# First stage of the spectral branch: kernel half rounded before signal half from row 4 on, last two rows convolved one by one

## The chip, the cores and the metric

One core of a Trainium2 chip runs the whole program. The metric is the device time in microseconds of one execution; the number given is the median of several runs.

## What is computed

The input `x` has 2048 rows (sequence) of 576 channels. Four layers follow each other, each added to its input after a layer norm: a Fourier mix (A), a gated state-space branch (B), A again, B again. B does not look at its input's layers at all beyond the gate: its expensive part depends on `k`, `v` and the weights only.

```python
def _A_ref(x, dft_seq_re, dft_seq_im, dft_hid_re, dft_hid_im):
    a = jnp.einsum("bsd,ed->bse", x, dft_hid_re)
    b = jnp.einsum("bsd,ed->bse", x, dft_hid_im)
    return jnp.einsum("ts,bse->bte", dft_seq_re, a) - jnp.einsum("ts,bse->bte", dft_seq_im, b)

def _B_ref(q, k, v, shift_k, ssm_k, ssm_D):
    k_pad = jnp.pad(k, ((0, 0), (ks - 1, 0), (0, 0)))
    k_shift = sum(k_pad[:, t:t + S, :] * shift_k[:, ks - 1 - t] for t in range(ks))   # ks = 4
    kv = k_shift * v
    y = irfft(rfft(kv, 2 * S) * rfft(ssm_k, 2 * S))[:S] + kv * ssm_D
    return q * y

x = x + _A_ref(_layernorm(x), ...)
x = x + _B_ref(_layernorm(x), ...)
x = x + _A_ref(_layernorm(x), ...)
x = x + _B_ref(_layernorm(x), ...)
```

## The kernel before

**The main line.** Each A layer is two rounds of matrix products on TensorE. In the first layer (`layer`) the sequence product runs over 128 steps: for each of 4 blocks of output rows and 2 matrices (cosine, sine), 16 steps over the contraction. One step multiplies the normalised rows by one 128x512 tile of the DFT matrix. Every fp32 number is carried as a rounded part and a remainder, so a step is 12 products into four accumulators `s` and 2 into `rm`. The tile of the DFT matrix arrives by a DMA from SyncE's queue (L171), ScalarE rounds it (`mats<-flts`, L101) and VectorE subtracts to get the remainder (`mats<-flts,mats`, L102). This last one is called a C split below. Two steps are prepared ahead.

**The branch.** The B layers share one inverse and forward transform of `k_shift * v` and `ssm_k`. It runs between the steps of the first layer, as a generator (`branch`) that the main loop advances by a few pieces per step. The positions are 16 rows `j` of 128x576 numbers each. The first stage, which the change touches, does for each row:

- the signal half: convolve `k` with the four taps of `shift_k` (`convolve`, L397 multiplies and L402 adds, two rows at a time on a 128x1152 view, 7 operations for a pair), multiply by the row of `v` (L430), round on ScalarE (`f1r<-f1f`, L101), subtract on VectorE (`f1r<-f1f,f1r`, L102);
- the kernel half: the row of `ssm_k` is loaded (L422), rounded (`f1r<-flts`, L101) and subtracted (`f1r<-flts,f1r`, L102);
- from row 4 on, one set of products for both halves: three visits (`f1_products`), each 6 matmuls of 128x384 into two of three PSUM banks `bf`, then two ScalarE copies out of the banks (L455, called evacuations below) and a store to DRAM from ScalarE's queue (L456).

**What sets the order.** `todo` lists (row, half) in the order in which the halves are rounded; 1 is the kernel half, 0 the signal half. Rows 0 to 3 do all kernel halves, then all signal halves. From row 4 on it goes signal, kernel, signal, kernel. Each entry gives two slots in the main loop. The convolution's operations are spread over these slots: `left` is the number of operations that must be done before the next signal half, divided by the slots until then. `f1_loads` asks for the rows of `v` and `ssm_k` three entries ahead, into a ring of three buffers (`land`): a load waits until the entry three places before it has been read for the last time. The three visits of a row follow the rounding of its second half. On top of this a scheduler places the instructions of each engine; every engine, and SyncE's queue of loads too, then works strictly in that order.

The rest of the program (hidden product, middle stage of the branch, the third layer with Strassen's scheme, the gates) is not touched.

Of the kernel before, what the change touches and what calls it, by code (L numbers as in the profile page):

```python
# [13 lines left out]
OP = mybir.AluOpType  # L14
# [4 lines left out]
D = 576  # L19
J = S // P  # L20
# [11 lines left out]
K_FIRST = 4  # L32
# [22 lines left out]
KR = 4  # L55
# [13 lines left out]
def fnet_h3_kernel(ctx: ExitStack, tc: tile.TileContext, x, c_mat, w_re, w_im, k_pad, v, shift_k,  # L69
                   ssm_k, ssm_d, f1c, i2c, midc, out):  # L70
    nc = tc.nc
# [28 lines left out]
    def split(h, l, src):  # L100
        a = nc.scalar.activation(h, src, AF.Copy).ins  # L101
        return a, nc.vector.tensor_tensor(l, src, h.bitcast(F32), OP.subtract).ins  # L102
# [31 lines left out]
    def lay(t, at, *sizes):  # L134

        for name, words, n in sizes:
            ring.setdefault(name, Ring()).tiles.extend(t[:, at + i * words:at + (i + 1) * words] for i in range(n))
            at += n * words
        assert at <= t.shape[1], (at, t.shape, sizes)
        return at  # L140
# [5 lines left out]
    def two(v):  # L146
        return v.rearrange("p (a n) -> p a n", a=2)
# [198 lines left out]
    def parts(i):  # L346
        v = ring[i]()
        return v[:, :D], v[:, D:]
# [4 lines left out]
    def branch():  # L353
# [3 lines left out]
        at = lay(flts, SC_AT + CRAW * NT, ("so", D, 4), ("land", D, 3))  # L357
# [3 lines left out]
        ks = f1f[:, :KR * 2 * D]  # L361
        lay(f1f, KR * 2 * D, ("wt", 2 * D, 2), ("rp", 2 * D, 2))
        tmp = f1f[:, 8 * 2 * D:]
        wt, rows, landed, fcs, paired = [], {}, {}, {}, []
        k_loaded = [0]

        def load_w4():
            for i in range(2):
                t = two(ring["wt"]())
                nc.sync.dma_start(t, bass.AP(tensor=shift_k.tensor, offset=shift_k.offset + 2 * i * D,  # L370
                                             ap=[[0, P], [D, 2], [1, D]]))
                wt.extend(t[:, i, :].unsqueeze(1).broadcast_to([P, 2, D]) for i in range(2))

        def load_k(upto):
            while k_loaded[0] < min(upto, (J + 4) // 2):
                i = k_loaded[0]
                at = i % KR * 2 * D
                nc.sync.dma_start(ks[:, at:at + 2 * D], k_pad[:, 2 * i * D:2 * (i + 1) * D])
                k_loaded[0] += 1

        def k_rows(row):

            at = row % (2 * KR) * D
            if at + 2 * D <= KR * 2 * D:
                return [(slice(0, 2), two(ks[:, at:at + 2 * D]))]
            return [(slice(n, n + 1), ks[:, o:o + D].unsqueeze(1)) for n, o in ((0, at), (1, 0))]

        def convolve():
            for i in range(J // 2):
                if not wt:  # L390
                    load_w4()
                load_k(i + KR - 1)
                rp = rows[i] = two(ring["rp"]())
                for t in range(4):
                    out_t = two(tmp) if t else rp
                    for n, k in k_rows(2 * i + t):
                        nc.vector.tensor_tensor(out_t[:, n], k, wt[3 - t][:, n], OP.mult)  # L397
                    yield
                    if t == 1:
                        load_k(i + KR)  # L400
                    if t:
                        nc.vector.tensor_tensor(rp, rp, out_t, OP.add)  # L402
                        yield

        todo = [(1, 1), (0, 1)] + [(j, 1) for j in range(2, K_FIRST)] + [(j, 0) for j in range(K_FIRST)]
        todo += [(j, src) for j in range(K_FIRST, J) for src in range(2)]
        loads = [0]

        def f1_loads(upto):
            while loads[0] < min(upto, len(todo)):  # L410
                j, src = todo[loads[0]]
                loads[0] += 1
                if j not in fcs:
                    fcs[j] = two(ring["fc"]())
                    if pows:
                        load_fr(fcs[j], f1c[j])
                    else:
                        raw = two(tmp[:, :2 * P])
                        nc.sync.dma_start(raw, f1c[j])
                        nc.scalar.activation(fcs[j], raw, AF.Copy)  # L420
                landed[j, src] = ring["land"]()
                nc.sync.dma_start(landed[j, src], (ssm_k if src else v)[:, j, :])  # L422
                if src and j == 0:
                    nc.sync.dma_start(tmp[:1, D:], ssm_d[None, :])

        def f1_split(j, src):
            r = landed.pop((j, src))
            if not src:
                row = rows[j // 2][:, j % 2, :]
                nc.vector.tensor_tensor(row, row, r, OP.mult)  # L430
                r = row
            elif j == 0:
                nc.vector.tensor_tensor(r[:1], r[:1], tmp[:1, D:], OP.add)
            if j < K_FIRST:
                xf = parts("xf")
                parted[:] = split(xf[0], xf[1], r)
                return xf
            if not src:
                t = ring["xp"]()
                paired[:] = t[:, :2 * D], t[:, 2 * D:]  # L440
            h, l = (t.rearrange("p (a s d) -> p a s d", a=2, s=2)[:, :, src, :] for t in paired)
            parted[:] = split(h, l, two(r))
            return tuple(paired)

        def f1_products(j, fc, xf, at, n, so, to):
# [10 lines left out]
            nc.scalar.dma_start(t_d[:, j::J, to:to + n], so)  # L456

        conv, made_ops, visits = convolve(), 0, []
        def visit(half):
            if visits and visits[0][0] <= half:  # L460
                f1_products(*visits.pop(0)[1:])

        for n, (j, src) in enumerate(todo):
            f1_loads(n + 1)
            if n < 2:
                yield
            xf = f1_split(j, src)
            if j < K_FIRST:
                visits += [(2 * n + 2, j, fcs[j], xf, hf * HD, HD, "so", hf * D + src * HD) for hf in range(2)]
            elif src:  # L470
                visits += [(2 * n + 3, j, fcs[j], xf, at, VW, "sp", at) for at in range(0, 2 * D, VW)]
            if n:
                f1_loads(n + 3)
            later = [m for m in range(n + 1, len(todo)) if todo[m][1] == 0 and 7 * (todo[m][0] // 2 + 1) > made_ops]
            for half in range(2):
                visit(2 * n + half)
                if later and n > 2:
                    left = 7 * (todo[later[0]][0] // 2 + 1) - made_ops
                    for _ in range(-(-left // (2 * (later[0] - n) - half)) if left > 0 else 0):
                        next(conv)  # L480
                        made_ops += 1
                yield
# [6 lines left out]
        at = lay(m1, 0, ("df", 2 * D, 3), ("mc", 4 * P, 1))  # L489
# [6 lines left out]
        at = lay(m1, at, ("yf", D, 2))  # L496
        fc_at = at
        at = lay(flts, SC_AT + CRAW * NT, ("res", D, 2))
# [267 lines left out]
    pending = []  # L766
    lay(flts, SC_AT, ("craw", NT, CRAW))
    br = branch()
    wl = load_w()
    load_x(0)  # L770
# [29 lines left out]
    for n, whole in layer(get_x0, lambda j: x[:, j, :], done0, pending):  # L800
        part = whole == "part"
        if part:
            whole = False
        if (whole or whole is not None and n % J < J - 1) and n <= F1_END and not part:
            at = n if whole else n - 0.5
# [27 lines left out]
        m = n - PREP  # L833
# [207 lines left out]
    for n, whole in layer(get_x1, lambda j: xb_d[j], done1, pending, 1):  # L1041
# [12 lines left out]
        if n == STATIC:  # L1054
            t7.append(region_a(FR, "t7"))
            at = lay(flts, SC_AT + CRAW * NT, ("csum", WIDE, 3), ("rems", 2 * REM, 2))
# [128 lines left out]
```

## Time and profile before

| | |
|---|---|
| median of 3 runs | 1179.39 us (1178.54 to 1179.56) |
| the profiled execution | 1178.94 us, of which 1177.0 us are the span from its first to its last instruction |
| TensorE matmul busy | 1165.9 us |
| VectorE busy | 867.8 us |
| ScalarE busy | 647.8 us |
| granted TensorE clock | 0.999 |

The first stage of the branch runs from the first microseconds to about 197 us; the rows with 384 columns, from row 4 on, take from about 92 us to 196 us. `PE` is the matmul part of TensorE, `PEld` its weight loads, `DVE` VectorE, `ACT` ScalarE, `SP` SyncE; `SPq` and `ACTq` are instructions of their queues, mostly DMA issues. A line of a timeline gives the start, the duration from the first start to the last end of a run of equal instructions, and in brackets the engine's idle time before it with what ended it.

### The profile page before, as it was taken

The numbers are of one execution on the slowest core, as the hardware profiler recorded it, in microseconds if no ns is written. First come the engines' busy times: TensorE is split into PE (matmuls) and PEld (weight loads), VectorE is DVE, ScalarE is ACT, GpSimd is POOL, SyncE is SP. The second block draws the span as 40 slices with busy tenths as digits, with TensorE's granted clock in tenths as the row PEclk, the third lists the DMA queues.
The fourth block names the chain that finished last, engine by engine and source line by source line (L and its number), as shares of the span: only waits on it lengthen the run. The fifth ranks groups of instructions, "written<-read, shape, count | busy, mean of one in ns | idle before, by whom it ended". The sixth has DMA issues, their size and how long they took to land.

```text
span 1177.0 us, 18134 instructions
## 1 busy us (share of the span) xinstructions
PE 1165.9 (99%) x6198; PEld 989.8 (84%) x6198; DVE 867.8 (74%) x1564; ACT 647.8 (55%) x1280; POOL 75.7 (6%) x115
## 2 busy tenths in 40 slices
PE   9999999999999999999999999999999999999997
PEld 6776667988899988898888898888888888889997
DVE  7899984688787788877757666866685777774674
ACT  8865655567766667766645667434434445450210
POOL 2310000000000000001101111000000000001111
PEclk9999999999999999999999999999999999999999
DMA  9879898546766766749966777772762877894531
GB/s 326 298 232 306 270 300 284 164 139 178 214 206 192 210 181 191 193 135 258 272 197 216 249 245 239 239 238 89 251 240 73 251 262 257 265 332 149 194 111 41
DMA packets 147453, 255.64 MB, mean 217 GB/s; under 512 B 16161, under 2 KB 56353, under 8 KB 147362
## 3 DMA queue, kind: packets, MB, share of 16 engines
q1 hardware_dynamic: 111890, 210.17, 56.6%
q10 hardware_dynamic: 28560, 37.91, 9.1%
q0 software_dynamic: 6912, 6.43, 2.4%
q8 instruction: 48, 0.79, 0.3%
q14 instruction: 43, 0.35, 0.1%
HBM read 187.80 MB, written 66.65 MB: 216 GB/s over the span
## 4 chain that ended last, share of the span: by engine, by line
PE 93%; DVE 2%; DMA 2%; ACT 1%; issue 1%; SPq 0%; POOL 0%; DVEq 0%; ACTq 0%
PE s L78 54%; PE bk L78 31%; PE rm L78 6%; PE bf L78 2%; DMA t<-ud 1%; DVE f1f L397 1%; DMA vd<-flts 0%; DVE f1f L402 0%; DVE mats L102 0%; DMA early<-in_x 0%; ACT flts L516 0%; DMA flts<-vd 0%; DMA td<-flts 0%; DVE f1r L102 0%; ACT mid L516 0%
## 5 line engine op out<-in xcount | busy, mean ns | idle before, releaser
L78 PE MATMUL s<-mats 128*128 128x512 f32 x2102 | 548.0, 396 | 2.7 <-DVE mats L762 1.5
L78 PEld LDWEIGHTS s<-mats 128*128 128x128 f32 x2102 | 382.7, 189 | 83.8 <-issue 10.9
L102 DVE TENSOR_TENSOR mats<-flts,mats 128x512 fp32r<-128x512 f32 x206 | 140.9, 688 | 55.8 <-ACT mats L101 53.4
L101 ACT ACTIVATE mats<-flts 128x512 fp32r<-128x512 f32 x206 | 128.2, 628 | 79.9 <-PE bk L78 29.6
L516 ACT ACTIVATE flts<-bk 128x288 f32<-128x288 f32 (+1 forms) x192 | 78.4, 409 | 97.7 <-PE bk L78 85.2
L78 PE MATMUL bk<-mid 128*128 128x288 f32 x704 | 127.9, 298 | 0.7 <-DVE mid L522 0.4
L78 PEld LDWEIGHTS bk<-mid 128*128 128x128 f32 x704 | 111.2, 188 | 19.7 <-ACT flts L516 4.5
L78 PE MATMUL bk<-w,u 128*128 128x288 f32 x864 | 120.5, 295 | 0.2
L78 PEld LDWEIGHTS bk<-w,u 128*128 128x128 f32 x864 | 116.8, 188 | 2.4 <-ACT flts L516 1.4
L522 DVE TENSOR_TENSOR mid<-flts,mid 128x576 fp32r<-128x576 f32 (+1 forms) x149 | 92.5, 625 | 7.4 <-ACT mid L516 5.3
L78 PE MATMUL rm<-mats 128*128 128x512 f32 x304 | 94.7, 391 | 0.0
L516 ACT ACTIVATE mid<-flts 128x576 fp32r<-128x576 f32 (+1 forms) x148 | 79.5, 574 | 1.9 <-DMA flts<-vd 0.9
L78 PE MATMUL bk<-mats 128*128 128x288 f32 (+1 forms) x376 | 67.8, 317 | 0.0
L78 PEld LDWEIGHTS rm<-mats 128*128 128x128 f32 x304 | 56.9, 188 | 12.5 <-issue 0.3
L455 ACT ACTIVATE flts<-bf 128x384 f32<-128x384 f32 (+1 forms) x104 | 43.2, 462 | 42.9 <-PE bf L78 40.5
L291 DVE TENSOR_TENSOR flts<-flts,bk 128x288 f32<-128x288 f32 x48 | 21.8, 454 | 60.6 <-PE bk L78 58.3
L78 PE MATMUL s<-t,mats 128*128 128x512 f32 x264 | 65.3, 390 | 0.3 <-DVE t L102 0.3
L188 POOL TENSOR_TENSOR flts<-flts 128x1 f32<-128x1 f32 x34 | 28.0, 824 | 517.0 <-DVE flts L187 517.0
L78 PE MATMUL bk<-mats,t 128*128 128x288 f32 (+1 forms) x368 | 59.3, 303 | 0.0
L78 PEld LDWEIGHTS s<-t,mats 128*128 128x128 f32 x264 | 49.4, 188 | 11.2 <-DVE t L102 0.8
L516 ACT ACTIVATE flts<-flts 64x288 f32<-64x288 f32 x128 | 56.7, 443 | 3.9
L78 PEld LDWEIGHTS bk<-mats 128*128 128x128 f32 x376 | 55.6, 188 | 3.4
(152 smaller groups left out, 1496.6 us busy)
## 6 DMA issues: line engine op xcount, KB each, us to landing
flts<-in_c_mat SPq DMA_DIRECT2D x148, 256.0 KB, 3.5
ph<-in_c_mat SPq DMA_DIRECT2D x54, 512.0 KB, 4.4
flts<-in_c_mat SPq DMA_DIRECT2D x30, 512.0 KB, 5.2
flts<-td SPq DMA_DIRECT2D x53, 288.0 KB, 3.1
td<-flts ACTq DMA_DIRECT2D x36, 384.0 KB, 4.5
vd<-flts ACTq DMA_DIRECT2D x64, 144.0 KB, 3.1
flts<-vd SPq DMA_DIRECT2D x32, 288.0 KB, 4.1
ud<-ph ACTq DMA_DIRECT2D x12, 512.0 KB, 6.4
```

The source lines that it names most:

```text
L78: return nc.tensor.matmul(ps, lhsT, rhs, start=first, stop=last, skip_group_check=more).ins
L101: a = nc.scalar.activation(h, src, AF.Copy).ins
L102: return a, nc.vector.tensor_tensor(l, src, h.bitcast(F32), OP.subtract).ins
L188: pows.append(nc.gpsimd.tensor_tensor(rs, ve, mhalf, OP.pow).ins)
L291: added[:] = [nc.vector.tensor_tensor(r[:, cs], r[:, cs], ps[:, :HD], OP.add).ins]
L397: nc.vector.tensor_tensor(out_t[:, n], k, wt[3 - t][:, n], OP.mult)
L455: stored[:] = [nc.scalar.activation(so[:, i, :], ps[i], AF.Copy).ins]
L516: last_act.append(nc.scalar.activation(*args, **kw).ins)
L522: nc.vector.tensor_tensor(l, src, h.bitcast(F32), OP.subtract)
```

## The change

Four edits in `branch`:

- in `todo`, from row 4 on the kernel half stands ahead of the signal half of the same row;
- `f1_split` takes its new buffer with the kernel half, and the three visits of a row are entered with the signal half, which now comes second. They stand at the same place in the list as before;
- the convolution of rows 14 and 15 is done row by row on 128x576 views (`k_row`, the loop over `part`), 14 operations where there were 7;
- `conv_ops` gives the number of operations that a row needs: 7 per pair as before up to row 13, then 56 for row 14 and 63 for row 15. It takes the place of `7 * (j // 2 + 1)`.

```diff
+        def k_row(row, part):
+            at = (row + part.start) % (2 * KR) * D
+            return [(part, ks[:, at:at + D].unsqueeze(1))]
+
         def convolve():
             for i in range(J // 2):
...
                 rp = rows[i] = two(ring["rp"]())
-                for t in range(4):
-                    out_t = two(tmp) if t else rp
-                    for n, k in k_rows(2 * i + t):
-                        nc.vector.tensor_tensor(out_t[:, n], k, wt[3 - t][:, n], OP.mult)
-                    yield
-                    if t == 1:
-                        load_k(i + KR)
-                    if t:
-                        nc.vector.tensor_tensor(rp, rp, out_t, OP.add)
+                for part in (slice(0, 2),) if i < J // 2 - 1 else (slice(0, 1), slice(1, 2)):
+                    for t in range(4):
+                        out_t = two(tmp) if t else rp
+                        for n, k in k_rows(2 * i + t) if part.stop - part.start == 2 else k_row(2 * i + t, part):
+                            nc.vector.tensor_tensor(out_t[:, n], k, wt[3 - t][:, n], OP.mult)
                         yield
+                        if t == 1:
+                            load_k(i + KR)
+                        if t:
+                            nc.vector.tensor_tensor(rp[:, part], rp[:, part], out_t[:, part], OP.add)
+                            yield
+
+        def conv_ops(j):
+            return 7 * (j // 2 + 1) if j < J - 2 else 7 * (J // 2 + j - J + 2)
 
-        todo += [(j, src) for j in range(K_FIRST, J) for src in range(2)]
+        todo += [(j, src) for j in range(K_FIRST, J) for src in (1, 0)]
...
-            if not src:
+            if src:
                 t = ring["xp"]()
                 paired[:] = t[:, :2 * D], t[:, 2 * D:]
...
-            elif src:
+            elif not src:
                 visits += [(2 * n + 3, j, fcs[j], xf, at, VW, "sp", at) for at in range(0, 2 * D, VW)]
...
-            later = [m for m in range(n + 1, len(todo)) if todo[m][1] == 0 and 7 * (todo[m][0] // 2 + 1) > made_ops]
+            later = [m for m in range(n + 1, len(todo)) if todo[m][1] == 0 and conv_ops(todo[m][0]) > made_ops]
...
-                    left = 7 * (todo[later[0]][0] // 2 + 1) - made_ops
+                    left = conv_ops(todo[later[0]][0]) - made_ops
```

**ScalarE, around row 8's signal half.** `f1r<-f1f` is the rounding of the signal half of row 8, `f1r<-flts` that of its kernel half, `flts<-bf` an evacuation, `mats<-flts` the rounding of a DFT tile. (Line 455 of before is line 463 of the changed kernel, 456 is 464, 430 is 438, 402 is 407, 397 is 402.) Before:

```order
L101 ACTIVATE f1r<-flts 128x2x288
L456 DMA td<-flts 256x1x384
L455 ACTIVATE flts<-bf_66 128x384
L101 ACTIVATE f1r<-f1f 128x2x288
L455 ACTIVATE flts<-bf_68 128x384
L101 ACTIVATE mats<-flts 128x512
L456 DMA td<-flts 256x1x384
```

With the change:

```order
L101 ACTIVATE f1r<-flts 128x2x288
L464 DMA td<-flts 256x1x384
L463 ACTIVATE flts<-bf_66 128x384
L463 ACTIVATE flts<-bf_68 128x384
L101 ACTIVATE mats<-flts 128x512
L101 ACTIVATE f1r<-f1f 128x2x288
L464 DMA td<-flts 256x1x384
```

The signal half's rounding moved from between the two evacuations of one visit to behind both, and behind a DFT tile's rounding.

**ScalarE, around row 7's kernel half.** Before:

```order
L455 ACTIVATE flts<-bf_67 128x384
L101 ACTIVATE mats<-flts 128x512
L101 ACTIVATE f1r<-flts 128x2x288
L456 DMA td<-flts 256x1x384
L455 ACTIVATE flts<-bf_66 128x384
L455 ACTIVATE flts<-bf_68 128x384
L101 ACTIVATE mats<-flts 128x512
L456 DMA td<-flts 256x1x384
L101 ACTIVATE f1r<-f1f 128x2x288
```

With the change:

```order
L463 ACTIVATE flts<-bf_67 128x384
L101 ACTIVATE mats<-flts 128x512
L101 ACTIVATE f1r<-flts 128x2x288
L101 ACTIVATE f1r<-f1f 128x2x288
L464 DMA td<-flts 256x1x384
L463 ACTIVATE flts<-bf_68 128x384
L463 ACTIVATE flts<-bf_66 128x384
L101 ACTIVATE mats<-flts 128x512
```

Row 7's signal half now stands ahead of the two evacuations of row 6's first visit; before it stood behind them.

**VectorE, from row 6's kernel half to row 7's multiplication by `v`.** `f1r<-flts,f1r` is row 6's kernel half, `f1r<-f1f,f1r` its signal half, `mats<-flts,mats` a C split, 128x1152 rows are the convolution. Before, where row 6's multiplication is the first row and row 7's the one but last:

```order
L430 TENSOR_TENSOR f1f<-f1f,flts 128x576
L397 TENSOR_TENSOR f1f<-f1f 128x1152 x2
L102 TENSOR_TENSOR f1r<-f1f,f1r 128x2x288
L102 TENSOR_TENSOR mats<-flts,mats 128x512
L102 TENSOR_TENSOR f1r<-flts,f1r 128x2x288
L402 TENSOR_TENSOR f1f<-f1f 128x1152
L102 TENSOR_TENSOR mats<-flts,mats 128x512
L397 TENSOR_TENSOR f1f<-f1f 128x1152
L430 TENSOR_TENSOR f1f<-f1f,flts 128x576
L402 TENSOR_TENSOR f1f<-f1f 128x1152
```

With the change:

```order
L102 TENSOR_TENSOR f1r<-flts,f1r 128x2x288
L102 TENSOR_TENSOR mats<-flts,mats 128x512
L438 TENSOR_TENSOR f1f<-f1f,flts 128x576
L402 TENSOR_TENSOR f1f<-f1f 128x1152
L102 TENSOR_TENSOR f1r<-f1f,f1r 128x2x288
L402 TENSOR_TENSOR f1f<-f1f 128x1152
L438 TENSOR_TENSOR f1f<-f1f,flts 128x576
L102 TENSOR_TENSOR mats<-flts,mats 128x512
```

Row 6's kernel half moved ahead of its multiplication, and row 7's multiplication follows row 6's after three operations in place of six.

## The prediction

> **What bounds the kernel now.** I read the page first, then stretches of the stage that the change touches, then the waits in it.
>
> ```profile
> span 1177.0 us, 18134 instructions
> PE 1165.9 (99%) x6198; PEld 989.8 (84%) x6198; DVE 867.8 (74%) x1564; ACT 647.8 (55%) x1280; POOL 75.7 (6%) x115
> PE 93%; DVE 2%; DMA 2%; ACT 1%; issue 1%; SPq 0%; POOL 0%; DVEq 0%; ACTq 0%
> ```
>
> TensorE holds 93% of the chain that ended last and is idle for 1177.0 - 1165.9 = 11.1 us of the whole span. The change removes no matmul, so it can only win idle time back, and only the idle time of its own stage. Five stretches, with the columns length, PE, weight loads, VectorE, ScalarE, GpSimd, clock, DMA share, GB/s:
>
> ```profile
> 50.00:90.00 40.00, 40.00 (x199) 29.95 (x198) 36.79 (x59) 26.39 (x55) 4.74 (x8) 1.00 0.70 213
> 90.00:130.00 40.00, 39.56 (x201) 27.13 (x199) 40.00 (x46) 22.32 (x45) 2.12 (x4) 1.00 0.97 313
> 130.00:170.00 40.00, 40.00 (x203) 27.78 (x200) 37.23 (x45) 25.30 (x52) 1.59 (x3) 1.00 0.85 272
> 170.00:197.00 27.00, 27.00 (x137) 18.82 (x136) 9.98 (x15) 15.08 (x32) 0.53 (x1) 1.00 0.85 273
> 601.00:652.00 51.00, 51.00 (x227) 42.23 (x226) 35.64 (x86) 29.20 (x57) 6.51 (x12) 1.00 0.65 209
> ```
>
> From 90 to 130 us VectorE has not one free moment (40.00 of 40.00) and the DMA engines are 97% taken; there TensorE loses 0.44 us. From 170 us on VectorE works 9.98 of 27 us. So the stage has two limits close together, TensorE and VectorE, and the waits of the stage (86 to 200 us) say who is late:
>
> ```profile
> ACT f1r L101 <- DMA flts<-in_ssm_k: 4.7, 2, 2.4
> ACT f1r L101 <- DVE f1f L430: 2.1, 5, 1.0
> DVE f1f L430 <- DMA flts<-in_v: 1.0, 1, 1.0
> PE bf L78 <- ACT flts L455: 0.3, 1, 0.3
> ```
>
> ScalarE stands still for a late row of `ssm_k` twice and for the multiplication by `v` five times. It works in order, so the evacuations behind these are late, and TensorE waits for a PSUM bank. Busy time hides most of such a wait, because a matmul's start and end overlap; the distance between starts shows it. The PE timeline, four places:
>
> ```profile
> 94.70 1.40 PE L78 MATMUL s<-mats 128*128 128x512 f32 x5
> 96.03 0.79 PE L78 MATMUL bf<-f1r 64*128 64x384 f32 x6
> ...
> 98.71 1.39 PE L78 MATMUL s<-mats 128*128 128x512 f32 x5
> 100.09 0.79 PE L78 MATMUL bf<-f1r 64*128 64x384 f32 x6
> ...
> 108.87 1.66 PE L78 MATMUL s<-mats 128*128 128x512 f32 x6
> 110.67 0.79 PE L78 MATMUL bf<-f1r 64*128 64x384 f32 x6
> ...
> 118.28 1.66 PE L78 MATMUL s<-mats 128*128 128x512 f32 x6
> 120.24 0.79 PE L78 MATMUL bf<-f1r 64*128 64x384 f32 x6 [0.30 <-ACT flts L455]
> ...
> 127.87 1.66 PE L78 MATMUL s<-mats 128*128 128x512 f32 x6
> 129.46 0.79 PE L78 MATMUL bf<-f1r 64*128 64x384 f32 x6
> ```
>
> Undisturbed, a visit starts 129.46 - 127.87 = 1.59 us after the six matmuls ahead of it began. At 110.67 it is 1.80, at 120.24 it is 1.96; with five matmuls 1.33 at 96.03 and 1.38 at 100.09. Lost: 0.21, 0.37 and 0.05 us, 0.63 together, and the other 33 visits of this width keep the undisturbed distance. **0.63 us is all that the change can win here**, 0.05% of the time.
>
> **The change part by part.** First the two larger losses. ScalarE at both places:
>
> ```profile
> 109.06 0.69 ACT L101 ACTIVATE f1r<-flts 128x576 fp32r<-128x576 f32 x1 [2.37 <-DMA flts<-in_ssm_k]
> 109.74 0.87 ACT L455 ACTIVATE flts<-bf 128x384 f32<-128x384 f32 x2
> ...
> 118.39 0.49 ACT L455 ACTIVATE flts<-bf 128x384 f32<-128x384 f32 x1 [1.57 <-PE bf L78]
> 119.13 0.69 ACT L101 ACTIVATE f1r<-f1f 128x576 fp32r<-128x576 f32 x1 [0.25 <-DVE f1f L430]
> 119.72 0.47 ACT L455 ACTIVATE flts<-bf 128x384 f32<-128x384 f32 x1
> ```
>
> *Row 8 (the 0.37 us).* The rounding of the signal half stands between the two evacuations of a visit and costs 119.72 - 119.13 = 0.59 us plus its wait of 0.25. In the new order it stands behind both, so this loss goes: -0.37 us. Row 5's rounding stood between two evacuations too and now stands behind them; with its products' inputs earlier in VectorE's queue, I count the 0.05 us as gone.
>
> *Row 7 (the 0.21 us).* The kernel half waited for `ssm_k` until 109.06. Its load now has a buffer earlier (its place in the ring frees with row 5's multiplication, which was row 6's before), so that wait goes. But row 7's signal half now stands ahead of the same two evacuations, and it needs the multiplication by `v`. That row of `v` has the ring place of row 6's kernel half, and this is where the price lies. When is the place free, and when is the row wanted? VectorE has no gap here, so its queue can be counted by distances between starts:
>
> ```profile
> 77.45 1.34 DVE L402 TENSOR_TENSOR f1f<-f1f 128x1152 f32<-128x1152 f32 x1
> 78.72 0.68 DVE L102 TENSOR_TENSOR mats<-flts,mats 128x512 fp32r<-128x512 f32 x1
> 79.33 1.34 DVE L397 TENSOR_TENSOR f1f<-f1f 128x1152 f32<-128x1152 f32 x1
> 80.59 0.75 DVE L430 TENSOR_TENSOR f1f<-f1f,flts 128x576 f32<-128x576 f32 x1
> 81.26 1.34 DVE L402 TENSOR_TENSOR f1f<-f1f 128x1152 f32<-128x1152 f32 x1
> ...
> 101.78 0.74 DVE L430 TENSOR_TENSOR f1f<-f1f,flts 128x576 f32<-128x576 f32 x1
> 102.55 0.33 SPq L422 DMA_DIRECT2D flts<-in_ssm_k  x1
> ```
>
> 1.27 us for 1152 columns, 0.61 for a C split, 0.67 for 576 columns. The two VectorE orders are equal up to the split at 78.72; from there to the end of row 6's kernel half the new order holds as much work as the old one to the end of row 6's multiplication, 23.1 us in both. That multiplication ended at 101.78 + 0.74 = 102.52, so the new load can be issued at 102.5 us, the moment at which the load of 102.55 went out. From the kernel half's end to row 7's multiplication stand a split, a multiplication, a convolution row, row 6's signal half and another convolution row: 0.61 + 0.67 + 1.27 + 0.67 + 1.27 = 4.5 us. The row is wanted at 107.0 us. How long do these loads take? First all loads of `v` and `ssm_k` between 85 and 175 us, then those of 101.5 to 108 us (least, median, most):
>
> ```profile
> DMA to landing us min/median/max: 2.8/4.5/7.2
> ...
> DMA to landing us min/median/max: 6.1/6.3/6.5
> ```
>
> With 4.5 us VectorE does not wait, the rounding is over at 107.0 + 0.75 + 0.59 = 108.3 us, before the visit of 108.15 has ended, and the loss is 0. With 7.2 us the row lands at 109.7; multiplication 0.75, rounding 0.59, both evacuations as before (110.67 - 109.74 = 0.93): the next visit at 111.97 in place of the undisturbed 108.87 + 1.59 = 110.46, a loss of 1.5 us. I take 6.3 us, since the same moment of the same stretch shows it and the traffic moved there (one load of each kind, the same stores) is alike: landing 108.8, visit at 111.1, loss 0.6 us where there was 0.21: **+0.4 us**. VectorE stands idle for 108.8 - 107.0 = 1.8 us.
>
> [...]
>
> *Those 1.8 us later on.* VectorE's queue holds the C splits of the main line. Counted the same way, the splits of steps 22 to 40 stand 0.6 to 3.8 us nearer to the head than before (one of them at no difference; steps 20 and 21 stand 0.7 us farther back), so being 1.8 us late mostly uses up that advantage, and from 170 us on 17 of 27 us are free. Rows 9 and 10, with 5.7 and 5.0 us between buffer and multiplication, can hold an evacuation again: between 0 and 0.6 us, I take 0.1.
>
> *Rows 14 and 15 one by one.* Six 1152-column operations become twelve of 576: 6 x (2 x 0.67 - 1.27) = 0.4 us more VectorE work. Their last products had time to spare:
>
> ```profile
> 179.47 0.75 DVE L102 TENSOR_TENSOR f1r<-flts,f1r 128x576 fp32r<-128x576 f32 x1
> ...
> 189.85 0.79 PE L78 MATMUL bf<-f1r 64*128 64x384 f32 x6
> ```
>
> Row 15's inputs were complete at 180.2 us, its first visit came at 189.85, 9.6 us later, and the free 17 us of VectorE lie around it. Nothing on the path; without that cover it would be the 0.4 us.
>
> *Loads.* SyncE's queue carries the same loads; each stands where its buffer comes free in both orders, and no DFT tile stands behind a load whose buffer frees later by more than 1 us. 0. The matmul order is the same from the last visit on.
>
> Sum: -0.37 - 0.05 + 0.4 + 0.1 = +0.1 us, from a profiled execution of 1178.94 us (span 1177.0 and 1.94 around it). The median of the runs shown, 1179.39, is 0.45 above that execution. **Forecast: 1179.4 us, no change.** 0.2%, 2.4 us, is about what a measurement of this kernel can tell from no change.
>
> **The rivals.** *All three losses go.* If the row of `v` lands by 107.5 us, the sum is -0.63 + 0.1: 1178.9 us. For it: ScalarE's place for every signal half but row 7's is now behind the visit's evacuations. Against it: the 6.1 us. This too is within 0.2%.
>
> *The late `v` becomes the bound (slower).* From row 4 on `v` has a buffer one entry later than before and is wanted by VectorE, behind whose queue everything stands; `ssm_k`, which won the time, held up ScalarE alone. If the loads take 7.2 us, rows 7, 9 and 10 each hold their visit by up to 1.5 us and each wait adds to the next one's start: 4.5 - 0.42 - 0.21 = +3.9, 1183.3 us. It decides from two such rows on (over 2.4 us). Against it: 4.5 us median, and the VectorE queue that gets shorter ahead of the later rows. Rows 13 to 15 also have under 4 us, but ScalarE's place there leaves 5 us.
>
> *Room inside a busy TensorE (faster).* If the 40.00 of 40.00 hid more idle time than the starts show, better order could win several us, say 3: 1176.4 us. Against it: the visits at equal distances above. [...]
>
> **How the numbers follow.** Forecast (traded losses) 0.45; all losses go 0.31; late `v` 0.18; hidden room 0.06. The first two are both no change: same 0.76, slower 0.18, faster 0.06. Range: from 1178.2 (all losses go, with the half microsecond by which runs of this kernel differ) to 1181.8, half way into the late case; the likeliest alone has 1178.6 to 1180.4.
>
> **What would show it.** Right: ScalarE's `f1r<-f1f` no longer between evacuations; no wait for `ssm_k` at 109 us, but VectorE waiting one to two microseconds for `in_v` near 107 us; PE's visits near 110 us late by about 0.6 us and the one near 120 us undisturbed. The forecast is wrong if PE's losses between 86 and 200 us add up to over 3 us, if C splits are waited for, or if time moves outside this stage.

## The result and the profile after

The changed kernel takes 1184.16 us (median of 6 runs, 1183.66 to 1185.7) where the kernel before takes 1179.39 (median of 6, 1178.39 to 1180.01): 1.0043 times as long, 95% interval 1.003 to 1.0056. That is slower by 4.8 us, outside the predicted range and on the side that had 0.18. The page of the profiled execution after the change, its span, its TensorE row and its chain:

```profile
span 1182.0 us, 18143 instructions
PE 1167.1 (99%) x6198; PEld 991.5 (84%) x6198; DVE 869.7 (74%) x1570; ACT 647.8 (55%) x1280; POOL 75.5 (6%) x115
PE 95%; DMA 2%; ACT 1%; DVE 1%; issue 0%; SPq 0%; POOL 0%; DVEq 0%; ACTq 0%
```

The span grew by 5.0 us, TensorE's busy time by 1.2 only, with the same 6198 matmuls. So some 4 us are new idle time. The first two of the prediction's stretches again, after the change:

```profile
50.00:90.00 40.00, 36.66 (x180) 27.11 (x179) 35.54 (x56) 24.99 (x55) 4.63 (x8) 0.97 0.68 211
90.00:130.00 40.00, 40.00 (x190) 28.12 (x190) 35.02 (x40) 19.79 (x41) 1.81 (x5) 0.95 0.82 266
```

Before, TensorE was busy for 40.00 of 40 us from 50 to 90; now for 36.66, with 180 matmuls in place of 199. The clock column, 1.00 in both stretches before, shows 0.97 and 0.95, and from 90 to 130 TensorE is busy without a break and yet does 190 matmuls in place of 201. There are two losses, then: a wait, and slow matmuls. The PE timeline after the change shows both:

```profile
83.02 0.67 PE L78 MATMUL bf<-f1r 64*128 64x288 f32 x6
83.61 1.21 PE L78 MATMUL s<-mats 128*128 128x512 f32 x4
88.16 1.09 PE L78 MATMUL bf<-f1r 64*128 64x288 f32 x6 [3.34 <-ACT flts L463]
...
90.62 1.05 PE L78 MATMUL rm<-mats 128*128 128x512 f32 x2
91.47 4.18 PE L78 MATMUL s<-mats 128*128 128x512 f32 x12
95.49 0.62 PE L78 MATMUL rm<-mats 128*128 128x512 f32 x2
```

The second 288-wide visit of row 3 comes at 88.16, after a wait of 3.34 us for an evacuation on ScalarE. Behind it two matmuls take 1.05 us in place of the usual 0.62 (last row), and twelve 4.18. The clock there, in stretches of 4 us (columns as in the prediction):

```profile
84.00:88.00 4.00, 0.82 (x4) 0.34 (x2) 4.00 (x6) 1.18 (x3) 0.00 (x0) 0.92 0.77 264
88.00:92.00 4.00, 3.84 (x13) 2.98 (x14) 2.20 (x4) 2.03 (x6) 0.53 (x1) 0.50 0.37 113
92.00:96.00 4.00, 4.00 (x15) 3.15 (x14) 4.00 (x6) 0.62 (x1) 0.00 (x0) 0.73 0.86 265
```

It falls to half with the wait and is back at 1.00 from 96 us on. What held ScalarE? Its timeline, after:

```profile
81.33 0.63 ACT L101 ACTIVATE mats<-flts 128x512 fp32r<-128x512 f32 x1
86.82 0.68 ACT L101 ACTIVATE f1r<-flts 128x576 fp32r<-128x576 f32 x1 [4.86 <-DMA flts<-in_ssm_k]
87.42 0.69 ACT L463 ACTIVATE flts<-bf 128x288 f32<-128x288 f32 x2
```

and the same engine before the change:

```profile
81.37 0.69 ACT L101 ACTIVATE f1r<-f1f 128x576 fp32r<-128x576 f32 x1 [0.21 <-DVE f1f L430]
84.82 0.71 ACT L455 ACTIVATE flts<-bf 128x288 f32<-128x288 f32 x2 [2.76 <-PE bf L78]
...
92.12 0.69 ACT L101 ACTIVATE f1r<-flts 128x576 fp32r<-128x576 f32 x1 [2.37 <-DMA flts<-in_ssm_k]
```

Row 5's kernel half has its turn on ScalarE at 92.12 - 2.37 = 89.75 in the old order and at 81.33 + 0.63 = 81.96 in the new one: 7.8 us earlier. There it waits 4.86 us for its row of `ssm_k`, and behind it, in the same in-order queue, stand the two evacuations of a visit (83.02) that was over at 83.02 + 0.67 = 83.69. Before, only the signal half of row 3 stood ahead of those evacuations (81.37), with a wait of 0.21. When did the load go out? First VectorE's row that frees its ring place (row 3's multiplication by `v`), then SyncE's row, after the change:

```profile
79.65 0.74 DVE L438 TENSOR_TENSOR f1f<-f1f,flts 128x576 f32<-128x576 f32 x1
```

```profile
80.42 1.14 SPq L430 DMA_DIRECT2D flts<-in_ssm_k  x1
```

The place is free at 80.39 and the load is issued at once, but that is 1.5 us ahead of its use, and it lands 6.4 us later, when the rounding starts. Before the change it was issued at 89.05, 0.7 us ahead of its place on ScalarE, and took 3.0 us; only a visit that had just begun stood behind it.

**The sum.** Undisturbed, as in a run shown below (84.67 - 83.76 = 0.91 for three matmuls, 3 x 0.227 + 0.23), the visit starts at 83.61 + 4 x 0.227 + 0.23 = 84.75. It started at 88.16: 3.4 us. From there to the two matmuls at 95.49 it is 7.33 us where an undisturbed run needs 4.59: 2.7 us more. Together 6.2 us. The same matmul of the main line starts 6.0 us later than before at 198 us and 5.0 us later at the end: 1.0 us comes back at 1022 to 1033 us, where the old execution loses 0.55 us at one matmul that waits for VectorE and smaller amounts beside it, and the new one loses nothing. The two losses are the result.

### The profile page after: what moved, and what is told of

It reads as the page before. It is cut to its first block, busy times and chain, and to the rows that moved or that the text cites. A ratio compares the mean times of both kernels' runs of the same rounds, so it can differ in the third digit from the quotient of the medians.

```text
span 1182.0 us, 18143 instructions
## 1 busy us (share of the span) xinstructions
PE 1167.1 (99%) x6198; PEld 991.5 (84%) x6198; DVE 869.7 (74%) x1570; ACT 647.8 (55%) x1280; POOL 75.5 (6%) x115
## 4 chain that ended last, share of the span: by engine, by line
PE 95%; DMA 2%; ACT 1%; DVE 1%; issue 0%; SPq 0%; POOL 0%; DVEq 0%; ACTq 0%
PE s L78 56%; PE bk L78 31%; PE rm L78 6%; PE bf L78 3%; DMA td<-flts 1%; DMA flts<-in_ssm_k 1%; DMA vd<-flts 0%; DMA early<-in_x 0%; ACT flts L524 0%; DMA flts<-vd 0%; ACT flts L463 0%; DVE mats L102 0%; ACT mid L524 0%; DVE f1f L407 0%; DVE flts L185 0%
```

## The experiments

**Theory A**: row 5's rounding waits on ScalarE for its `ssm_k` ahead of two evacuations, and the wait lowers the clock. **Rival B**: the last rows' convolution one by one. **Rival C**: late rows of `v`, or VectorE. Four kernels on one chip, beside 30 runs of the kernel before (median 1179.17).

**The convolution alone** (old order of the halves, the rest of the change kept):

```diff
-        todo += [(j, src) for j in range(K_FIRST, J) for src in (1, 0)]
+        todo += [(j, src) for j in range(K_FIRST, J) for src in range(2)]
...
-            if src:
+            if not src:
...
-            elif not src:
+            elif src:
```

> The changed kernel with the old order of the halves (signal first) and rows 14 and 15 still convolved one by one. Theory A (ScalarE's rounding of row 5's kernel half waits for its ssm_k row ahead of an evacuation, and TensorE's clock falls in the wait): this part is innocent, 1179.4 us within 0.7. Rival B (the row-by-row convolution costs the time): 1183 to 1185 us.

Measured: 1179.2 us, ratio 0.9999 (0.9989 to 1.0008), no wait of TensorE over 0.4 us between 50 and 200 us. The convolution costs nothing that can be measured. Rival B falls.

**The order of the halves alone** (the rows convolved in pairs, as before):

```diff
-                for part in (slice(0, 2),) if i < J // 2 - 1 else (slice(0, 1), slice(1, 2)):
+                for part in (slice(0, 2),):
...
-            return 7 * (j // 2 + 1) if j < J - 2 else 7 * (J // 2 + j - J + 2)
+            return 7 * (j // 2 + 1)
```

> The changed kernel with rows 14 and 15 convolved as a pair again, kernel half first from row 4 on. Theory A: the whole loss stays, 1183.5 to 1185 us, with one TensorE wait of 3 to 4 us near 84 us and matmuls at half clock behind it. Rival B: 1179.4 us.

Measured: 1182.98 us, ratio 1.0029 (1.0019 to 1.0039), nine runs from 1180.01 to 1184.04. ScalarE and TensorE in this kernel's timeline:

```profile
86.69 0.69 ACT L101 ACTIVATE f1r<-flts 128x576 fp32r<-128x576 f32 x1 [4.35 <-DMA flts<-in_ssm_k]
```

```profile
88.02 0.66 PE L78 MATMUL bf<-f1r 64*128 64x288 f32 x6 [2.83 <-ACT flts L463]
...
90.00 4.36 PE L78 MATMUL s<-mats 128*128 128x512 f32 x12
```

The same wait, half a microsecond shorter, and again slow matmuls behind it. The wait lies 0.2 us and the time half a microsecond below the ranges that I had given; the interval overlaps with that of the whole change (1.003 to 1.0056). The loss belongs to the order of the halves.

**One instruction moved**: the change as it is, with the rounding of row 5's kernel half issued behind the last evacuation:

```diff
-            parted[:] = split(h, l, two(r))
+            with behind(*(stored if src and j == 5 else ())):
+                parted[:] = split(h, l, two(r))
```

> The changed kernel, but the rounding of row 5's kernel half is issued behind the last evacuation of row 3; loads, buffers and VectorE's work stay. Theory A: ScalarE's 4.9 us wait no longer stands ahead of an evacuation, TensorE's 3.3 us wait and the slow clock go, 1178.3 to 1179.5 us. Rival C (the rows of v come late and VectorE, or the DMA queues, pay all along the rows): that is not touched, 1182.5 us or more.

Measured: 1178.8 us, ratio 0.9997 (0.9987 to 1.0007). ScalarE, then TensorE:

```profile
83.87 0.71 ACT L464 ACTIVATE flts<-bf 128x288 f32<-128x288 f32 x2 [1.75 <-PE bf L78]
...
87.10 0.69 ACT L101 ACTIVATE f1r<-flts 128x576 fp32r<-128x576 f32 x1 [0.51 <-DMA flts<-in_ssm_k]
```

```profile
83.76 0.98 PE L78 MATMUL s<-mats 128*128 128x512 f32 x3
84.67 0.66 PE L78 MATMUL bf<-f1r 64*128 64x288 f32 x6
85.26 1.20 PE L78 MATMUL s<-mats 128*128 128x512 f32 x4
86.29 0.62 PE L78 MATMUL rm<-mats 128*128 128x512 f32 x2
86.75 2.90 PE L78 MATMUL s<-mats 128*128 128x512 f32 x12
89.49 0.62 PE L78 MATMUL rm<-mats 128*128 128x512 f32 x2
```

The load lands as late as before (the rounding starts at 87.10, after 86.82), but the evacuations are ahead of it now and TensorE doesn't wait. These rows are the undisturbed case used above: from the visit at 84.67 to 89.49 it is 4.82 us with four matmuls behind the visit, 4.59 with three. All of the loss is gone with one dependency more. It moves that rounding, and the scheduler then moves some neighbours: the visit starts one matmul earlier, and VectorE and SyncE do a few of their operations in another order, mostly from 102 us on. Rival C falls as well: VectorE's waits for rows of `v` add up to 3.2 us in this kernel and to 3.6 in the changed one, and yet the time is back.

**The change from row 6 on only**, rows 4 and 5 in the old order:

```diff
-        todo += [(j, src) for j in range(K_FIRST, J) for src in (1, 0)]
+        todo += [(j, src) for j in range(K_FIRST, J) for src in ((1, 0) if j >= 6 else (0, 1))]
...
-            if src:
+            if src == (1 if j >= 6 else 0):
...
-            elif not src:
+            elif src == (0 if j >= 6 else 1):
```

> The changed kernel with rows 4 and 5 signal first as before, kernel half first only from row 6 on. Theory A: row 5's ssm_k has its old buffer place, no TensorE wait over 1 us near 84 us, 1178.3 to 1179.7 us. Rival C: ten of twelve rows keep the late v, 1182 us or more.

Measured: 1180.01 us, ratio 1.0005 (0.9996 to 1.0015), 0.3 us above the range that I had given; the longest wait of TensorE between 50 and 200 us is 0.5. VectorE's waits for rows of `v` come to 8.5 us here, and cost nothing that can be measured. What costs is the change at rows 4 and 5.

**Is the load itself the cause?** The orders of TensorE, VectorE and ScalarE were kept row for row, and only the length of row 5's load was changed, with row 6's as a control; 13 runs of the kernel before beside them (median 1179.69). The edit for 16 of 576 columns (288 for the half, row 6 in place of 5 for the control):

```diff
-                nc.sync.dma_start(landed[j, src], (ssm_k if src else v)[:, j, :])
+                nc.sync.dma_start(landed[j, src][:, :16 if (j, src) == (5, 1) else None],
+                                  (ssm_k if src else v)[:, j, :16 if (j, src) == (5, 1) else None])
```

> The changed kernel, every engine's order of instructions as it is, but of row 5's ssm_k only 16 of 576 columns are loaded (the rest of the place keeps the row of v that was there before), so that part of the output is computed from other data. Theory A (the landing of this one load is the whole loss): it lands 2 to 4 us after its issue in place of 6.4, ScalarE's wait ahead of the rounding of row 5's kernel half is under 2 us in place of 4.9, TensorE waits under 1.2 us near 85 us, the clock there stays at 1.00, and the time is 1178.5 to 1180.5. Rival F (it is the order on ScalarE or VectorE, whatever the load takes): 1183 to 1185.

> As the kernel with 16 columns, but with half of row 5's ssm_k, 288 of 576 columns; the other half keeps what was in its place, so that part of the output is computed from other data. Theory A with the landing set by bytes: 4 to 5 us after the issue, TensorE's wait 1 to 2.5 us, and the time between the two: 1180 to 1182.5, at the upper end if the clock still falls. If the landing is set by what stands ahead in the DMA queues and not by this load's own bytes, it lands 6 us after its issue and the time is 1183 to 1185.

> Control: the changed kernel with 16 of 576 columns of row 6's ssm_k loaded in place of row 5's, so that part of the output is computed from other data. Theory A: row 6's rounding stands ahead of no late evacuation, so the wait near 88 us and the slow clock stay: 1183 to 1185. Rival G (any load less in this full stretch of the DMA engines helps alike): 1179 to 1181.

Measured: 16 columns 1181.85 us, ratio 1.0017 (1.0007 to 1.0026); half a row 1183.81, 1.0039 (1.0024 to 1.0054); the control 1184.61, 1.0043 (1.0026 to 1.006). My numbers for 16 columns were missed, and Rival F's 1183 to 1185 did not come there either; the control came as Theory A had it, and Rival G falls. The view of DMA issues for the kernel with 16 columns says why it was missed (KB of one, us from issue to landing):

```profile
flts<-in_ssm_k SPq DMA_DIRECT2D x1, 8.0 KB, 5.6
```

A load of 8 KB takes 5.6 us here, one of 144 KB 5.3, one of 288 KB 6.4: its own bytes hardly set the landing. The DMA share reads 0.98 to 1.04 from 80 to 84 us in these kernels. In the packets of the changed kernel's trace, the first of the 128 of row 5's `ssm_k` starts at 83.42, 3.0 us after the issue, with a DMA share of 0.97 in between, and a packet takes 93 ns; before the change the first started 1.55 us after the issue, with a share of 0.75. That the load waits for what is ahead of it in the DMA engines is my reading of these numbers; no run shows it by itself. But the three kernels still measure the chain, since the landing moved a little. Rounding on ScalarE and the visit behind it on TensorE, with 16 columns:

```profile
85.77 0.68 ACT L101 ACTIVATE f1r<-flts 128x576 fp32r<-128x576 f32 x1 [4.06 <-DMA flts<-in_ssm_k]
```

```profile
87.11 0.66 PE L78 MATMUL bf<-f1r 64*128 64x288 f32 x6 [2.53 <-ACT flts L463]
```

with half a row:

```profile
85.67 0.68 ACT L101 ACTIVATE f1r<-flts 128x576 fp32r<-128x576 f32 x1 [3.75 <-DMA flts<-in_ssm_k]
```

```profile
87.00 1.09 PE L78 MATMUL bf<-f1r 64*128 64x288 f32 x6 [2.23 <-ACT flts L463]
```

and in the control:

```profile
87.08 0.68 ACT L101 ACTIVATE f1r<-flts 128x576 fp32r<-128x576 f32 x1 [5.15 <-DMA flts<-in_ssm_k]
```

```profile
88.41 0.79 PE L78 MATMUL bf<-f1r 64*128 64x288 f32 x6 [3.62 <-ACT flts L463]
```

In these three, in the changed kernel and in the one with the halves' order alone, the visit starts 1.33 or 1.34 us after the rounding starts, whenever the load lands between 85.7 and 87.1 us. Over these 1.4 us the landing sets TensorE, one to one. The half row also shows the second loss by itself: its wait is the shortest, 2.23 us, and yet it is 2.0 us slower than the 16 columns with 2.53. Its visit takes 1.09 us, where the other's takes the normal 0.66, so the clock fell earlier there (0.83 from 84 to 88 us, 1.00 with 16 columns) and the slow stretch was longer: 7.54 us from the visit to the two `rm` matmuls that come 17 matmuls behind it, where 4.59 is undisturbed, 3.0 us more.

**Row 4's kernel half earlier**, to move the load of row 5:

```diff
-        todo = [...] + [(j, 1) for j in range(2, K_FIRST)] + [(j, 0) for j in range(K_FIRST)]
-        todo += [(j, src) for j in range(K_FIRST, J) for src in (1, 0)]
+        todo = [...] + [(j, 1) for j in range(2, K_FIRST)] + [(j, 0) for j in range(K_FIRST - 1)] + [(K_FIRST, 1), (K_FIRST - 1, 0), (K_FIRST, 0)]
+        todo += [(j, src) for j in range(K_FIRST + 1, J) for src in (1, 0)]
```

> The changed kernel with one more move: row 5 or 4 apart, the kernel half of row 4 is prepared ahead of the signal half of row 3, so that the multiplication that frees the landing place of row 5's ssm_k comes at another time, while the rounding of row 5's kernel half still stands ahead of the last evacuation of a 288-wide visit on ScalarE. Theory A (what counts is when that load's place frees against ScalarE's place for the rounding): if the load is issued 3 us or more before the place it holds now, TensorE's wait for an evacuation near 88 us is under 1 us, the clock stays at 1.00 and the time is 1178.5 to 1180.5; if it is issued no earlier, the wait of 2 to 4 us stays and the time is 1182.5 to 1185.5. Rival E (any order with the kernel half first on ScalarE from here on loses, whatever the load does): 1183 to 1185 with the load early too.

Measured: 1180.39 us, ratio 1.0014 (1.0004 to 1.0023). The load goes out at 79.93, half a microsecond earlier only, so neither condition of Theory A was met, and the visit waits for another thing:

```profile
87.86 0.66 PE L78 MATMUL bf<-f1r 64*128 64x288 f32 x6 [1.41 <-DVE f1r L102]
```

It waits 1.41 us for its own products' input, and the clock stays at 1.00 in every 4 us from 76 to 100. The run says nothing on whether an earlier load would be enough; Rival E's 1183 to 1185 did not come.

**What a wait does to the clock.** For this, another place was used: the kernel before, with ScalarE's rounding of eight C halves of the main line repeated (a C half is one half of a loaded piece of the DFT matrix; the scheduler then orders the main line somewhat differently):

```diff
+REPEAT = {20: 14, 38: 17, 56: 20, 74: 23, 92: 26, 110: 30, 128: 34, 146: 40}
...
+        for _ in range(again):
+            nc.scalar.activation(c[:, 0], RAW[step][:, i, :], AF.Copy)
...
-            cs[h] = split_half(steps[h // 2], h % 2)
+            cs[h] = split_half(steps[h // 2], h % 2, REPEAT.get(h, 0))
```

> The kernel before, with ScalarE's rounding of eight C halves of the main line repeated 14, 17, 20, 23, 26, 30, 34 and 40 times, so that TensorE waits at up to eight places, longer at each; the output is the same. Theory A (a long wait of TensorE costs twice: itself, and then matmuls at half the rate): at the places where TensorE waits under 2 us the matmuls behind the wait stay near 227 ns for 512 columns and the time lost is the wait alone; at the places where it waits over 3 us, 8 to 14 matmuls behind the wait stand about 427 ns apart, the windows there grant 0.5 to 0.8, and each costs 2 to 4 us more than its wait. Rival D (the slow matmuls after row 5's wait come from something else of that moment, such as loads in flight or the pile of late evacuations): the matmuls behind waits of 3 us and more stay at 227 ns and the clock at 1.00.

Measured, in one execution: 1300.2 us. Two of the waits on TensorE's timeline, with what follows:

```profile
866.78 3.23 PE L79 MATMUL s<-t 128*128 128x512 f32 x6 [7.13 <-ACT t L102]
869.81 2.37 PE L79 MATMUL s<-mats,t 128*128 128x512 f32 x6
872.01 1.54 PE L79 MATMUL s<-t,mats 128*128 128x512 f32 x6
...
1147.69 3.23 PE L79 MATMUL s<-mats,t 128*128 128x512 f32 x6 [20.07 <-ACT mats L102]
1150.72 3.29 PE L79 MATMUL s<-t 128*128 128x512 f32 x12
1153.85 2.43 PE L79 MATMUL s<-mats,t 128*128 128x512 f32 x10
```

Six such matmuls take 6 x 0.227 = 1.36 us between starts. After a wait of 7.13 us the first six take 3.03 and the next six 2.20: 2.5 us lost beside the wait. After 20.07 us the first six take 3.03 and the next twelve 3.13 in place of 2.72: 2.1 us. The price does not grow with the wait; both lie in the 2 to 4 us that I expected, though after 20.07 us fewer than 8 matmuls were slow. A second kernel with shorter holds:

```diff
-REPEAT = {20: 14, 38: 17, 56: 20, 74: 23, 92: 26, 110: 30, 128: 34, 146: 40}
+REPEAT = {20: 12, 38: 7, 56: 6, 74: 7, 92: 6, 110: 17, 128: 10, 146: 8}
```

> As the ladder before, with shorter holds (the rounding of the same C halves repeated 12, 7, 6, 7, 6, 17, 10 and 8 times), for waits of TensorE between 0.5 and 2.5 us; the output is the same. From the runs so far: a wait of 1.41 us left the clock alone and one of 2.23 us halved the rate of the matmuls behind it. Expected: waits up to 1.4 us cost only themselves, waits of 2.2 us and more are followed by 8 to 14 matmuls 427 ns apart, and the border lies in between. Rival: the border isn't set by the wait's length alone, so that a shorter wait lowers the clock at one place and a longer one does not at another.

Measured, in one execution: 1195.19 us. Its timeline:

```profile
822.25 3.37 PE L79 MATMUL s<-mats,t 128*128 128x512 f32 x12 [1.24 <-ACT mats L102]
...
944.05 2.93 PE L79 MATMUL s<-mats 128*128 128x512 f32 x6 [3.44 <-ACT mats L102]
946.77 2.44 PE L79 MATMUL s<-t 128*128 128x512 f32 x9
...
979.49 0.74 PE L79 MATMUL s<-mats,u 128*128 128x512 f32 x2 [1.03 <-ACT mats L102]
980.07 0.40 PE L79 MATMUL bk<-mats,t 128*128 128x512 f32 x1
980.30 1.11 PE L79 MATMUL s<-mats,u 128*128 128x512 f32 x4
```

After 1.03 us the matmuls run on at 227 ns (980.30 - 980.07 = 0.23); after 1.24 the twelve lose under half a microsecond, one of them 472 ns long and none near 427 in a row; after 3.44 six stand 426 to 427 ns apart, fewer than the 8 to 14 that I expected, and the price is 1.6 us until they are back at 227. No wait of this kernel fell between 1.24 and 3.44 us, so the border was not found more closely. The waits of TensorE of 1 us and more with the matmuls behind them, counted one by one in the traces (the first 20 us are left out, and a wait of 3.60 us behind which TensorE stopped again after five matmuls):

| wait of TensorE, us | kernel | matmuls at about 427 ns behind it |
|---|---|---|
| 1.03, 1.24 | second ladder | none |
| 1.41 | row 4's kernel half earlier | none |
| 2.23 | half a row of `ssm_k` | 11 |
| 2.53 | 16 columns | 7 |
| 2.54 | first ladder | 11 |
| 2.83 | order of the halves alone | 7 |
| 3.34 | the change | 10 |
| 3.44 | second ladder | 6 |
| 3.62 | the control | 5 |
| 7.13, 9.43, 9.81, 11.57 | first ladder | 8, 9, 10, 5 |
| 13.81, 16.38, 20.07 | first ladder | 7, 8, 5 |

Rival D falls: in the ladders the slow matmuls follow waits of 2.54 to 20.07 us in the main line, with nothing of the branch stage near. The border lies between 1.41 and 2.23 us in these runs, and the number of slow matmuls doesn't follow the wait's length.

## Why the prediction was wrong

**What bounds the kernel** was read rightly: TensorE, with two limits close together in this stage.

**Rows 8 and 5: right.** The losses of 0.37 and of 0.05 us are gone: after the change all 384-wide visits keep the undisturbed distance but one, of row 12.

**Row 7: the mechanism right, the size not.** VectorE does wait for the late row of `v`, and it wants it when I said. SyncE's row of the load and VectorE's row of the multiplication, after:

```profile
108.88 0.33 SPq L430 DMA_DIRECT2D flts<-in_v  x1
```

```profile
113.83 0.76 DVE L438 TENSOR_TENSOR f1f<-f1f,flts 128x576 f32<-128x576 f32 x1 [0.50 <-DMA flts<-in_v]
```

Without its 0.50 us of wait it would have started 113.33 - 108.88 = 4.45 us after the issue; I had 4.5. But the load took 4.9 us and not the 6.3 that I chose, so the wait is 0.5 in place of 1.8, and the visits there keep the undisturbed distance (115.17 to 116.76, 1.59 us). +0.4 should have been -0.2. The 0.1 for rows 9 and 10 did not come either. What came in its place is a late `v` at row 13. VectorE's waits after the change, from 86 to 200 us, the longest of them with the row behind it, and row 12's first visit:

```profile
DVE f1f L438 <- DMA flts<-in_v: 3.6, 4, 1.9
```

```profile
166.70 0.76 DVE L438 TENSOR_TENSOR f1f<-f1f,flts 128x576 f32<-128x576 f32 x1 [1.88 <-DMA flts<-in_v]
167.37 0.75 DVE L102 TENSOR_TENSOR f1r<-f1f,f1r 128x576 fp32r<-128x576 f32 x1
```

```profile
168.23 0.80 PE L78 MATMUL bf<-f1r 64*128 64x384 f32 x6 [0.23 <-ACT mats L101]
```

Behind row 13's multiplication stands the subtraction of row 12's signal half, whose result row 12's visits read. It ends at 167.37 + 0.75 = 168.12, and the visit starts at 168.23, 0.3 us late. The profile names a rounding of ScalarE, which ended at 168.04; with the rounding of row 5 moved, the same visit is again 0.3 us late, 0.10 us behind the same subtraction and a wait of 1.90 us. So in the part of the stage that I looked at, the rival "all three losses go" was nearer than my forecast: 0.63 won, 0.3 lost. With row 5 out of the way the whole kernel shows it: 1178.8 us, as that rival had it (1178.9), though no measurement here tells it from no change.

**Rows 14 and 15 one by one: right**, hidden; shown by the kernel with that part alone.

**The step that failed is the one on the loads.** It says "The kernel half waited for `ssm_k` until 109.06. Its load now has a buffer earlier (…), so that wait goes", and later "*Loads.* … 0". For row 7 that holds. For row 5 the same edit moves the rounding 7.8 us ahead on ScalarE and its load 8.6 us ahead on SyncE, into a stretch where it takes 6.4 us in place of 3.0. I asked of each load whether its *buffer* came later than before, and what stood behind it on SyncE's queue; I did not ask what stands behind its *reader* on ScalarE. And I compared ScalarE's order only at the 384-wide visits, from row 4 on, though row 5's rounding now falls among the last 288-wide visits, of row 3. The trace of before had what was needed. In the new order row 3's multiplication follows the split at 78.72 directly, so the place is free at 79.33 + 0.75 = 80.1; with the landing of 6.3 us that I used for `v`, row 5 is rounded at 86.4, while the evacuations behind it are wanted at 84.8, as the old row at 84.82 shows. With the 1.33 us seen above from the rounding to the visit, the second visit of row 3, at 85.63 before, comes at 87.7: an estimate of 2.1 us. That alone would have made the forecast 1181.5, and not yet a clear loss.

**What I never priced is the clock.** The other step that was missing: 2.7 of the 6.2 us are matmuls at half rate behind the wait, a term that the sum did not have. Without them, and with the same 1.0 us coming back later, an estimate of the change's cost is 6.2 - 2.7 - 1.0 = 2.5 us, about 0.2%. The trace of before holds no wait of TensorE over 1.2 us between two matmuls, so no row of it could show this price. The runs show it: 427 ns for 512 columns in place of 227, for 5 to 11 matmuls behind a wait of 2.23 us or more. What sets the number of slow matmuls, no run here shows.

**The rivals.** The late `v` had the right side for a wrong reason: its mechanism is there, 3.6 us of VectorE's waits, but it cost TensorE the 0.3 us at row 12 alone. None named a rounding that waits for `ssm_k` ahead of evacuations. The sentence on what would make the forecast wrong ("if PE's losses between 86 and 200 us add up to over 3 us") is what happened, though nearly all of it lies before 96 us, at row 3's visit.

**Still open:** whether an earlier load alone would cure it. A fourth landing place, the direct test, wasn't tried. And the run with 16 columns spreads from 1180.26 to 1183.91, the order alone from 1180.01 to 1184.04. Waits near the border that lower the clock in some executions only would explain it; that is argued, not shown. The mean clocks of the executions lean that way and no more: with the order alone, 0.999 in the fastest and 0.996 to 0.998 in the others.

## What to carry to other kernels

When an edit moves an instruction forward in an in-order queue, follow the data it reads: issue plus landing time against its new place, for every row that it touches and first of all at the seam between two kinds of rows; and name what stands behind it in that queue. In these runs five waits of TensorE, from 2.23 to 20.07 us, cost 1.6 to 3.0 us each on top for the slow matmuls behind them; such a wait is to be priced with that. The cure can be one dependency: let the rounding follow the evacuations, and leave the rest of the new order as it is. Here it took back the whole loss and beat the kernel before by nothing that can be measured.

## What the runs showed of the hardware that was not expected

- A wait of 2.23 us halved the rate of the matmuls behind it (427 ns in place of 227 for 512 columns), one of 1.41 us did not; the price beside the wait, counted for five waits from 2.23 to 20.07 us, was 1.6 to 3.0 us, and no higher after the longest.
- A load of 8 KB took 5.6 us to land, one of 144 KB 5.3 and one of 288 KB 6.4, with a DMA share of 0.98 and more from 80 to 84 us: in that stretch the bytes hardly set the landing.
